# Output projection on 448 instead of 512 rows: two heads moved into the padding of the others by SBUF to SBUF transfers

## The chip, the cores and the metric

One core of one Trainium2 chip. The metric is the device time of one execution in microseconds (us), median of several. A ratio is the mean time of one kernel's fast runs over that of the other's fast runs of the same rounds, so it is not quite the ratio of the medians that are quoted beside it; the brackets after a ratio are its 95% interval.

## The reference

Two kinds of layer, each with a residual, applied as A, B, A, B to x of 2048 tokens by D = 448:

```python
def _A_ref(x, wqkv, wo):                     # on layernorm(x)
    H = 16; Dh = D // H                      # 16 heads of 28
    W, dil = 8, 2                            # 8 keys, every second token
    q, k, v = split(x @ wqkv)
    attn = softmax(where(mask, q . k[window] * Dh ** -0.5, -1e9))
    o = attn @ v[window]
    return o.reshape(B, S, D) @ wo           # the output projection

def _B_ref(x, w_gate, w_up, w_down):         # on layernorm(x), F = 1792
    return ((x @ w_gate) * (x @ w_up)) @ w_down
```

(cut and condensed; all data is bf16)

## The kernel before

The kernel keeps x in SBUF throughout. Heads have 28 rows, but a head sits in a slot of 32 partitions, so that the 16 heads fill four chunks of 128 partitions: `oT[128, 4, tokens]`. The four last rows of each slot are padding, and `wo_g` has zeros there. The output projection of a pair of 128-token blocks contracts half a chunk (64 rows) at a time; the two blocks work in the two halves of the array, crossed over after the first pass, so that each block gets all eight halves:

```python
wo_g = sb([128, 4, D], bf, "wo_g")
oT = sb([128, 4, HALF], bf, "oT")
...
memset("dve", wo_g[:], 0.0, "c_wo", 1000)
for j in range(4):
    dst = wo_g[32 * j:32 * j + DH, :, :]
    ...
# two blocks: 2 x 4 chunks x 2 halves = 16 matmuls of 64 x 128 by 64 x 448
twin_blocks(lambda w: ps[:, bk[w], 0:D],
            lambda w, c, lo: oT[lo:lo + 64, c, 128 * ((B + w) % 8):128 * ((B + w) % 8) + 128],
            lambda w, c, lo: wo_g[lo:lo + 64, c, :], ..., nd + WO, prio, bk)
```

The order of instructions on every engine is made when the kernel is built. A list scheduler simulates the engines with a table of durations and puts the instruction with the best priority next. The order then is fixed, and each engine is given its own instructions in it:

```python
def finish_of(self, key):
    ...
    if op.dma is not None:        # a transfer: the end of its issue, and its landing
        return max(o.end + o.lat for o in self.dgroup[(op.dma, op.mode)])
```

Two numbers of that table describe a transfer: what its issue takes on the queue, and its landing.

## Time and profile before

| | before |
|---|---|
| time, median (lowest to highest) of 3 | 394.73 us (393.76 to 395.34) |
| profiled span | 391.6 us |
| TensorE busy | 385.5 us, 98% |
| TensorE not busy | 391.6 - 385.5 = 6.1 us |
| granted clock, mean | 1.00 |
| issuing on the sync engine's queue, summed over the trace's records | 39.0 us of copies and loads, 98.9 us of transposes |

The prediction shows the lines that say what bounds it. One more view will be needed later, the busy time by stretches: start and end of the stretch, its length, the busy time of five engines (with the count of instructions), TensorE's granted clock, the share of the transfer engines, and GB/s. Of the kernel before:

```profile
30.00:40.00 10.00, 9.91 (x220) 5.34 (x218) 9.47 (x20) 8.38 (x17) 0.00 (x0) 1.00 0.08 20
60.00:100.00 40.00, 39.97 (x814) 23.48 (x811) 34.56 (x83) 27.14 (x55) 0.00 (x0) 1.00 0.23 43
```

TensorE has work all the time (9.91 of 10 and 39.97 of 40 us) and its clock is not lowered (1.00 in both). The weight loads are over by 30 us: the transfer engines' share falls to 0.08. By the trace's records the two matmuls of a pair start 3 to 4 ns apart and the next pair follows after 0.189 us at 448 columns and 0.216 us at 512 (97.4 to 98.4 us), while the record of one matmul is 349 or 376 ns long. From the last gate and up pair to the first matmul of an attention group it is 0.306 us where the next pair of its own kind follows after 0.21 us, so entering that mode costs about 0.09 us.

### The profile page before, as it was taken

The numbers are of one execution on the slowest core, as the hardware profiler recorded it, in microseconds if no ns is written. First come the engines' busy times: TensorE is split into PE (matmuls) and PEld (weight loads), VectorE is DVE, ScalarE is ACT, GpSimd is POOL, SyncE is SP. The second block draws the span as 40 slices with busy tenths as digits, with TensorE's granted clock in tenths as the row PEclk, the third lists the DMA queues.
The fourth block names the chain that finished last, engine by engine and source line by source line (L and its number), as shares of the span: only waits on it lengthen the run. The fifth ranks groups of instructions, "written<-read, shape, count | busy, mean of one in ns | idle before, by whom it ended". The sixth has DMA issues, their size and how long they took to land.

```text
span 391.6 us, 13910 instructions
## 1 busy us (share of the span) xinstructions
PE 385.5 (98%) x6142; PEld 214.1 (55%) x6142; DVE 271.0 (69%) x596; ACT 207.0 (53%) x398; POOL 7.8 (2%) x36
## 2 busy tenths in 40 slices
PE   8989999999999999999999999999999999999996
PEld 6645657655444544554556877444454544444674
DVE  5988999779957765784788644358932698467342
ACT  4788886578524745466742523368225772364130
POOL 6010000000000000000000000000000000000000
PEclk9999999999999999999999999999999999999999
DMA  8991143511221302210131151010150102402101
GB/s 274 300 288 34 21 92 32 97 24 28 49 49 28 77 7 56 42 28 13 17 49 27 30 95 29 25 23 8 26 118 5 23 7 56 88 3 20 31 25 47
DMA packets 53808, 22.47 MB, mean 57 GB/s; under 512 B 44837, under 2 KB 52853, under 8 KB 53749
## 3 DMA queue, kind: packets, MB, share of 16 engines
q1 hardware_dynamic: 52836, 19.47, 23.6%
q10 hardware_dynamic: 912, 2.12, 1.8%
q8 instruction: 48, 0.79, 0.8%
q14 instruction: 12, 0.09, 0.1%
HBM read 8.54 MB, written 2.71 MB: 29 GB/s over the span
## 4 chain that ended last, share of the span: by engine, by line
PE 98%; DVE 1%; issue 1%; DVEq 0%
PE ps L983 44%; PE ps L714 27%; PE ps L698 17%; PE ps L896 3%; PE ps L862 3%; PE ps L566 2%; PE ps L1004 1%; PE ps L660 1%; DVE xn_sb L651 0%; DVE x_sb L954 0%; DVEq L1084 0%; DVE O_sb L914 0%; DVE oT L937 0%; DVE O_sb L910 0%; DVE WQK L582 0%
## 5 line engine op out<-in xcount | busy, mean ns | idle before, releaser
L983 PE MATMUL ps<-xnTb,WGU 64*128 64x512 bf16 (+1 forms) x1960 | 180.4, 333 | 0.0
L983 PEld LDWEIGHTS ps<-xnTb,WGU 64*128 64x128 bf16 x1960 | 93.3, 94 | 72.9 <-ACT g_sb L989 1.5
L989 ACT ACTIVATE g_sb<-ps 128x512 bf16<-128x512 f32 (+1 forms) x140 | 71.4, 511 | 93.7 <-PE ps L983 93.1
L992 DVE TENSOR_TENSOR hT<-g_sb,ps 128x512 bf16<-128x512 bf16 (+1 forms) x140 | 79.2, 573 | 54.1 <-ACT g_sb L989 46.0
L714 PE MATMUL ps<-WD,hT 64*128 64x448 bf16 x840 | 84.0, 349 | 0.1
L714 PEld LDWEIGHTS ps<-WD,hT 64*128 64x128 bf16 x840 | 40.1, 94 | 36.9 <-DVE hT L992 0.7
L698 PE MATMUL ps<-xnTa,WQK 64*128 64x512 bf16 (+1 forms) x504 | 53.5, 353 | 0.3 <-DVE O_sb L914 0.2
L954 DVE TENSOR_TENSOR x_sb<-x_sb,ps 128x448 bf16<-128x448 bf16 x62 | 36.1, 612 | 25.2 <-PE ps L714 25.0
L630 DVE BATCH_NORM_STATS2 st<-x_sb 128x6 f32<-128x448 bf16 x64 | 37.4, 614 | 2.6 <-DMA x_sb<-in_A_x_dram 2.5
L869 ACT ACTIVATE E_sb<-ps 128x1024 bf16<-128x1024 f32 (+1 forms) x36 | 33.5, 980 | 9.8 <-PE ps L862 9.3
L750 ACT ACTIVATE qk<-ps 128x1024 bf16<-128x1024 f32 (+1 forms) x30 | 27.1, 921 | 19.3 <-PE ps L698 19.0
L651 DVE TENSOR_SCALAR xn_sb<-x_sb,mv,rstd 128x512 bf16<-128x512 bf16 (+1 forms) x64 | 33.6, 568 | 4.6 <-ACT rstd L635 4.6
L698 PEld LDWEIGHTS ps<-xnTa,WQK 64*128 64x128 bf16 x504 | 23.4, 94 | 24.0 <-ACT xnTa L666 0.8
L879 DVE TENSOR_TENSOR E_sb<-E_sb,MK 128x1024 bf16<-128x1024 bf16 (+2 forms) x40 | 23.9, 612 | 8.9 <-ACT E_sb L869 8.6
L714 PE MATMUL ps<-wo_g,oT 64*128 64x448 bf16 x256 | 29.1, 349 | 0.0
L633 ACT ACTIVATE lnv<-mv,eps_sb 128x2 f32<-128x2 f32 (+1 forms) x33 | 9.5, 293 | 30.5 <-DVE mv L632 30.2
L937 DVE TENSOR_TENSOR oT<-O_sb,R_sb 128x480 bf16<-128x480 f32 (+3 forms) x36 | 22.0, 625 | 3.4 <-ACT R_sb L926 3.1
L925 ACT ACTIVATE R_sb<-R_sb 128x480 f32<-128x480 f32 (+1 forms) x34 | 20.1, 601 | 5.7 <-DVE R_sb L924 5.7
L924 DVE STREAM_SHUFFLE R_sb<-O_sb 128x480 f32<-128x480 f32 (+1 forms) x34 | 22.6, 694 | 0.0
L698 PE MATMUL ps<-WV,xnTa 64*128 64x336 bf16 (+3 forms) x252 | 22.3, 304 | 0.2
L926 ACT ACTIVATE R_sb<-R_sb 128x480 f32<-128x480 f32 (+1 forms) x34 | 20.1, 602 | 0.3
L714 PEld LDWEIGHTS ps<-wo_g,oT 64*128 64x128 bf16 x256 | 12.3, 94 | 11.6 <-DVE oT L937 0.4
(47 smaller groups left out, 172.2 us busy)
## 6 DMA issues: line engine op xcount, KB each, us to landing
out_dram<-x_sb SPq DMA_DIRECT2D x15, 112.0 KB, 1.7
WD<-in_B_w_down_dram SPq DMA_DIRECT2D x2, 784.0 KB, 11.3
x_sb<-in_A_x_dram SPq DMA_DIRECT2D x3, 448.0 KB, 6.0
WGU<-in_B_w_up_dram SPq DMA_DIRECT2D x1, 896.0 KB, 18.0
WGU<-in_B_w_gate_dram ACTq DMA_DIRECT2D x1, 896.0 KB, 16.2
WGU<-in_B_w_up_dram SPq DMA_DIRECT2D x1, 672.0 KB, 17.8
WGU<-in_B_w_gate_dram ACTq DMA_DIRECT2D x1, 672.0 KB, 11.9
vt<-qk SPq DMA_DIRECT2D x42, 16.0 KB
```

Source lines behind the costliest of these rows:

```text
L630: sc.add("dve", one(lambda E, B=B: E.bn_stats(st6[:, B, :], x_sb[:, B, :]), ("bn", li, B)), 525.0, deps=[("x", li - 1, B)] + ([("xn", li - ...
L651: sc.add("dve", one(lambda E, B=B, dst=dst, src=src: E.tensor_scalar(dst, src, mv[:, B, 0:1], rstd[:, B:B + 1], ALU.subtract, ALU.mult), ( ...
L698: parts[0 if s < 3 else 1][1].append((lambda E, w=w, c=c, lo=lo, st=st, sp_=sp_: E.matmul(u["out"](w), u["lhs"](w, c, lo, lo + 64), u["rhs ...
L714: ins.append((lambda E, w=w, c=c, lo=lo, st=st, sp_=sp_: E.matmul(outs(w), lhs(w, c, lo), rhs(w, c, lo), start=st, stop=sp_), keys[w] if s ...
L750: return E.activation(dst, src, ACT.Copy) if hasattr(E, "activation") else E.tensor_copy(dst, src)
L869: return E.activation(E_sb[:, slot, 2 * hp:2 * hp + 2, 0:w], ps[:, b0:b0 + 2, 0:w], ACT.Exp, scale=SCALE)
L879: return E.tensor_tensor(e, e, m, ALU.mult)
L924: sc.add("dve", one(lambda E: E.stream_shuffle(R_sb[:, rs, 0:w], O_sb[:, os_, 0:w], [DH] * 32), ("Rs", li, qb)), dve_est(w) + 100.0, deps= ...
L954: sc.add("dve", one(lambda E: E.tensor_tensor(x_sb[:, B, :], x_sb[:, B, :], ps[:, bk[w], 0:D], ALU.add), ("x", li, B)), dve_est(D), deps=[ ...
L983: ins.append((lambda E, u=u, k=k, w=w: E.matmul(u["out"](w), WGU[64 * w:64 * w + 64, k, 128 * u["fc"]:128 * u["fc"] + 128], X[64 * w:64 * ...
L989: sc.add("act", one(lambda E, gs=gs, bk=bk: E.activation(g_sb[:, gs, 0:nt], ps[:, bk[0], 0:nt], ACT.Copy), ("G", li, j, fc)), act_est(nt), ...
L992: sc.add("dve", one(lambda E, gs=gs, bk=bk, fc=fc: E.tensor_tensor(hT[:, fc, hs, 0:nt], g_sb[:, gs, 0:nt], ps[:, bk[1], 0:nt], ALU.mult), ...
```

## The change

Intent: 448 rows need three and a half chunks, not four. Of chunk 3, half (two heads, 56 rows) is cut into pieces of 12 or 16 rows and moved by transfers into the padding rows of chunks 0 to 3 of the slots that remain; which half is moved depends on the parity w of the block, so that the two blocks of a pair still use different halves of the array. Each pair of blocks then takes 14 instead of 16 matmuls, 224 instead of 256 in all, for eight moves per pair, 128 in all. The core of the diff, with cuts marked:

```diff
+    MOVES = ((0, 0, 64, 16), (0, 32, 96, 16), (0, 64, 80, 12), (0, 96, 112, 12),   # w, slot, from row, rows
+             (1, 64, 0, 16), (1, 96, 32, 16), (1, 0, 16, 12), (1, 32, 48, 12))
-    wo_g = sb([128, 4, D], bf, "wo_g")
+    wo_g = sb([128, 2, 4, D], bf, "wo_g")            # one per parity, 16 loads instead of 4, no memset
-    twin_blocks(... oT[lo:lo + 64, c, ...], wo_g[lo:lo + 64, c, :], ..., nd + WO, prio, bk)
+    for n, (w, q, p0, k) in enumerate(MOVES):
+        dst = oT[q + DH:q + 32, 0:k // 4, m0 + 128 * w:m0 + 128 * w + 128]
+        src = oT[p0:p0 + k, 3, m0 + 128 * w:m0 + 128 * w + 128].unsqueeze(1)
+        sc.add("sp", one(lambda E, ...: E.dma_start(dst, src), ...), MVE, deps=nd, dma=f"d_m{p}", lat=MVL, ...)
+    for flip in (0, 1):
+        for c in range(4 - flip):                    # four halves, then three
+            ...
+    crossed(parts, [("OM", li, p)] + WO, prio, pe_cols(D), bk, "Yps")
+MVL = 2300.0                                         # the scheduler's table: landing of a move
+MVE = 330.0                                          # and its issue, ns
-PE_T = ("00", "01", "02", "03", "04")
+PE_T = ("00", "01", "02")                            # chunks of the first layer transposed on TensorE
...  (nearly every priority of the scheduler is new, the weights of the projection are loaded last,
...  some weight copies are bound to one engine, oT is a ring of 768 instead of 1024 tokens,
...  and the gate and up groups are kept in one fixed order)
```

More of the change, by code (lines that the diff above doesn't have):

```diff
@@ L28 @@
 MAIN = "R64"
-PE_T = ("00", "01", "02", "03", "04")
+PE_T = ("00", "01", "02")
 HEAD_LN = 5
-HEAD_P = (-53.71, -30.23, -20.33, -12.94, -19.33)
-HOLD_A = 1000.0
-HOLD_BA = 2000.0
-HOLD_BB = 500.0
+HEAD_P = (-25.07, -29.5, -27.33, -11.24, -8.12)
+HOLD_A = 0.0
+HOLD_BA = 1000.0
+HOLD_BB = 1000.0
 HOLD_N = 2
 S_EST = 270.0
-VX = 120.0
+VX = 0.0
 DPARTS = ((0, 7), (7, 14))
@@ L40 @@
 POOL_MASK = 0
-POOL_WQK = True
+WQK_ACT = ((0, 0), (0, 1), (2, 0))
 VFIRST = False
@@ L51 @@
 NBK = 8
-PR = {'AV': 8.84, 'rstd': -5.66, 'bn': 0.73, 'N': -2.82, 'Gps': -1.08, 'Tps': 16.85, 'H': 18.16, 'S': 10.61, 'VT': 19.61, 'Ex': 16.77, 'G': -2.93, 'xn': -6.19, 'QK': -6.56, 'Ddps': -26.52, 'V': 22.93, 'x': -0.84, 'lnv': -15.5, 'Oc': -6.51, 'Oa': -6.47, 'R': -19.3, 'VVps': 1.22, 'Yps': -25.3, 'PW': 58.69, 'T': -9.57, 'mv': 2.02, 'Rs': -2.57, 'Rl': 21.52, 'QKps': 4.71, 'E': -7.15, 'wqk': -9.31, 'wqp': -11.53}
-JP = {'A20': -3.02, 'B32': 16.28, 'B34': 16.21, 'A22': 20.13, 'B13': 2.73, 'A21': 6.27, 'B12': -2.81, 'A02': -0.21, 'A03': 4.03, 'B30': 4.3, 'B31': 8.23, 'B10': 21.86, 'B11': -14.15, 'A23': 29.86, 'A04': -0.79, 'B33': 153.62, 'A01': -5.33, 'B14': 4.53, 'A00': -24.6}
-XL = (2300.0, 2200.0, 4200.0, 5000.0, 5500.0)
+PR = {'lnv': 0.45, 'Yps': -0.46, 'Gps': 5.13, 'QK': 4.55, 'H': -5.95, 'R': -21.58, 'G': -8.35, 'VT': 8.79, 'S': -0.3, 'V': -1.49, 'Tps': 2.59, 'QKps': -8.74, 'T': 1.04, 'mv': -3.5, 'AV': -4.81, 'PW': 11.62, 'Oa': -19.68, 'bn': 1.23, 'N': -3.47, 'rstd': -11.91, 'Rl': -3.35, 'VVps': -4.87, 'x': -0.08, 'xn': -3.46, 'Ddps': -5.48, 'Ex': -6.97, 'E': 19.06, 'Rs': 1.63, 'Oc': 0.24, 'wqp': 2.97, 'wqk': 0.04}
+JP = {'A23': -34.68, 'B11': 4.55, 'B31': 13.93, 'A21': 15.34, 'A22': -41.14, 'B10': -17.89, 'A00': -1.57, 'B13': 1.34, 'B33': 15.35, 'A04': 3.4, 'A02': -1.01, 'A20': -93.26, 'B30': 0.09, 'B32': -5.05, 'A03': 22.53, 'B34': 1.96, 'A01': -0.42, 'B14': -9.92, 'B12': -2.11}
+XL = (3150.0, 4000.0, 4400.0, 5000.0, 5500.0)
 WVL = 5000.0
-STL = (2400.0, 2600.0, 2900.0, 2800.0)
-VONES_L = 18000.0
+STL = (2900.0, 3100.0, 3300.0, 3300.0)
+VONES_L = 15000.0
+MVL = 2300.0
+OW = 768
+WO_P = -43.2
+MVE = 330.0
 BL = (11000.0, 15000.0, 8000.0)
@@ L66 @@
 FILL = 30
-SEED = 190
+SEED = 557
 JITTER = 0
-ATT_P = 1.96
-A_CAP = 4
+ATT_P = 0.12
+A_CAP = 7
 B_CAP = 8
@@ L474, in build @@
     hT = sb([128, FC, 2, 512], bf, "hT")
-    oT = sb([128, 4, HALF], bf, "oT")
+    oT = sb([128, 4, OW], bf, "oT")
     ones32 = sb([128, 128], bf, "ones32")
@@ L488, in build @@
     sem_names += [f"d_t{li}_{j}" for li in range(4) for j in range(len(CH[li]))]
-    sem_names += [f"d_p{li}_{j}" for li in (0, 2) for j in range(len(CH[li]))] + [f"d_v{q}" for q in range(NQB)] + ["d_one", "d_stv"]
+    sem_names += [f"d_p{li}_{j}" for li in (0, 2) for j in range(len(CH[li]))] + [f"d_v{q}" for q in range(NQB)] + ["d_one", "d_stv"] + [f"d_m{p}" for p in range(NBLK // 2)]
     vt_all = nc.dram_tensor("vt", (256, S), bf, kind="Internal").ap()
@@ L498, in act_table_load, with plain_dma @@
         return E.add_instruction(atl)
-    def plain_dma(q, dst, src, key, sem, deps=(), lat=3000.0, prio=0.0, tmin=None):
-        sc.add(q, one(lambda E: E.dma_start(dst, src), key), {"sp": 520.0, "act": 500.0, "pool": 1000.0}[q], deps=deps, dma=sem, mode=0, lat=lat, prio=prio, tmin=tmin)
+    def plain_dma(q, dst, src, key, sem, deps=(), lat=3000.0, prio=0.0, tmin=None, est=None):
+        sc.add(q, one(lambda E: E.dma_start(dst, src), key), est or {"sp": 520.0, "act": 500.0, "pool": 1000.0}[q], deps=deps, dma=sem, mode=0, lat=lat, prio=prio, tmin=tmin)
     CH_ROWS = [0, 128, 192, 320]
@@ L533, in build @@
     memset("dve", eps_sb[:], EPS, "c_eps", 70)
-    memset("dve", wo_g[:], 0.0, "c_wo", 1000)
     sc.add("pool", one(lambda E: E.memset(ident[:], 1.0), "i_id"), 150, prio=-46)
@@ L574, in fn @@
                 return E.activation(dst, src, ACT.Copy) if hasattr(E, "activation") else E.tensor_copy(dst, src)
-            sc.add(("act", "dve", "pool") if POOL_WQK else ("act", "dve"), one(fn, ("wqk", c, w)), {"act": 470.0, "dve": 330.0, "pool": 600.0}, deps=[("stg", c), "c_wqk0"], prio=-28)
+            on_act = (c, w) in WQK_ACT
+            sc.add("act" if on_act else "dve", one(fn, ("wqk", c, w)), 560.0 if on_act else 300.0,
+                   deps=[("stg", c), "c_wqk0"] + ([("rstd", 0, int(WQK_ACT.index((c, w)) >= 1))] if on_act else []), prio=-28)
     for c in range(4):
@@ L588, in build @@
     ones_src = ones32[0:32, :].unsqueeze(1).to_broadcast([32, 16, 128])
-    plain_dma("sp", ones_dst, ones_src, ("vones",), "d_one", deps=["c_ones"], lat=VONES_L, prio=-40)
-    for j in range(4):
-        dst = wo_g[32 * j:32 * j + DH, :, :]
-        src = A_wo.rearrange("(c j e) d -> j e c d", c=4, j=4, e=DH)[j]
-        plain_dma("sp", dst, src, ("wo", j), "d_wo", deps=["c_wo"], lat=WOL, prio=-45)
+    plain_dma("sp", ones_dst, ones_src, ("vones",), "d_one", deps=["c_ones"], lat=3000.0, est=VONES_L, prio=-40)
+    MOVES = ((0, 0, 64, 16), (0, 32, 96, 16), (0, 64, 80, 12), (0, 96, 112, 12), (1, 64, 0, 16), (1, 96, 32, 16), (1, 0, 16, 12), (1, 32, 48, 12))
+    for j in range(8):
+        src = A_wo.rearrange("(c j e) d -> j e c d", c=4, j=4, e=DH)[j % 4]
+        plain_dma("sp", wo_g[32 * (j % 4):32 * (j % 4) + DH, j // 4, :, :], src, ("wo", j), "d_wo", lat=WOL, prio=WO_P)
+    for n, (w, q, p, k) in enumerate(MOVES):
+        r0 = DH * (12 + p // 32) + p % 32
+        plain_dma("sp", wo_g[q + DH:q + 32, w, 0:k // 4, :], A_wo[r0:r0 + k, :].rearrange("(r c) d -> r c d", r=4), ("wo", 8 + n), "d_wo", lat=WOL, prio=WO_P)
     for n, (k0, k1) in enumerate(KP):
@@ L599, in build @@
     WDR = [("wd", 0), ("wd", 1)]
-    WO = [("wo", j) for j in range(4)]
+    WO = [("wo", j) for j in range(16)]
     rings = {n: [None] * k for n, k in (("xn", NXN), ("o", NO), ("v", NV), ("v2", NV2), ("e", NE if PAIRED else 2 * NE), ("r", NR), ("g", NG))}
@@ L630, in ln_chunk @@
                 sc.add("dve", one(lambda E, B=B: E.bn_stats(st6[:, B, :], x_sb[:, B, :]), ("bn", li, B)), 525.0,
-                       deps=[("x", li - 1, B)] + ([("xn", li - 1, B)] if li else []), prio=prio)
+                       deps=[("x", li - 1, B)] + ([("xn", li - 1, B)] if li else []) + ([("mv", 0, 0)] if (li, B) == (0, 1) else []), prio=prio)
                 sc.add("dve", one(lambda E, B=B: E.bn_aggr(mv[:, B, :], st6[:, B, :]), ("mv", li, B)), 100.0, deps=[("bn", li, B)], prio=prio - 0.1)
@@ L927, in norm @@
         war = []
-        for B in range(tok // 128, (tok + nq - 1) // 128 + 1):
-            if B >= 8:
-                war.append(("Y", li, B - 8))
-            elif li >= 2:
-                war.append(("Y", li - 2, B + 8))
-        cut = [tok] + [HALF] * (tok < HALF < tok + nq) + [tok + nq]
+        g0 = S * (li // 2)
+        for p in range(tok // 256, (tok + nq - 1) // 256 + 1):
+            q = p + 8 * (li // 2) - OW // 256
+            if q >= 0:
+                war += [("Y", 2 * (q // 8), 2 * (q % 8)), ("Y", 2 * (q // 8), 2 * (q % 8) + 1)]
+        cut = [tok] + [t - g0 for t in range(0, 2 * S, OW) if tok < t - g0 < tok + nq] + [tok + nq]
         ins = []
@@ L936, in fn @@
             def fn(E, a=a, z=z):
-                return E.tensor_tensor(oT[:, :, a % HALF:a % HALF + z - a], O[:, :, a - tok:z - tok], R_sb[:, rs, 0:w].rearrange("p (h n) -> p h n", h=4)[:, :, a - tok:z - tok], ALU.mult)
+                m = (a + g0) % OW
+                return E.tensor_tensor(oT[:, :, m:m + z - a], O[:, :, a - tok:z - tok], R_sb[:, rs, 0:w].rearrange("p (h n) -> p h n", h=4)[:, :, a - tok:z - tok], ALU.mult)
             ins.append((fn, ("N", li, qb) if z == cut[-1] else None))
@@ L947, in y_blocks @@
                 nd.append(("N", li, qb))
-        twin_blocks(lambda w: ps[:, bk[w], 0:D], lambda w, c, lo: oT[lo:lo + 64, c, 128 * ((B + w) % 8):128 * ((B + w) % 8) + 128], lambda w, c, lo: wo_g[lo:lo + 64, c, :],
-                    (("Y", li, B), ("Y", li, B + 1)), [range(4)], [[]], nd + WO, prio, bk)
+        p, m0 = B // 2, (128 * B + S * (li // 2)) % OW
+        for n, (w, q, p0, k) in enumerate(MOVES):
+            dst = oT[q + DH:q + 32, 0:k // 4, m0 + 128 * w:m0 + 128 * w + 128]
+            src = oT[p0:p0 + k, 3, m0 + 128 * w:m0 + 128 * w + 128].unsqueeze(1)
+            sc.add("sp", one(lambda E, dst=dst, src=src: E.dma_start(dst, src), ("OM", li, p) if n == 7 else None), MVE, deps=nd, dma=f"d_m{p}", mode=li, lat=MVL, prio=prio + PR.get("OM", 0.0) * (n < 7))
+        parts = []
+        for flip in (0, 1):
+            ins = []
+            for c in range(4 - flip):
+                for h in (0, 1):
+                    w, lo = h ^ flip, 64 * h
+                    ins.append((lambda E, w=w, c=c, lo=lo, flip=flip: E.matmul(ps[:, bk[w], 0:D], oT[lo:lo + 64, c, m0 + 128 * w:m0 + 128 * w + 128], wo_g[lo:lo + 64, w, c, :],
+                                                                           start=c == 0 and flip == 0, stop=c == 2 and flip == 1),
+                                ("Y", li, B + w) if c == 2 and flip == 1 else None))
+            parts.append((flip, ins, []))
+        crossed(parts, [("OM", li, p)] + WO, prio, pe_cols(D), bk, "Yps")
         for w in range(2):
@@ L960, in build @@
     hslot_users = {}
+    gu_ops = []
     LASTB = [(int(b[1]), int(b[2])) for b in SEQ if b[0] == "B"][-1]
@@ L984, in b_chunk @@
                                                                  X[64 * w:64 * w + 64, k, c0:c0 + nt], start=k == 0, stop=k == 6), u["keys"][w] if k == 6 else None))
-            sc.add("pe", ins, 7 * pe_cols(nt), deps=u["deps"] + tdeps, mode=MAIN, prio=prio, acquire=u["bk"])
+            gu_ops.append(sc.add("pe", ins, 7 * pe_cols(nt), deps=u["deps"] + tdeps, mode=MAIN, prio=prio, acquire=u["bk"], after=gu_ops[-1] if gu_ops else None))
             for u in us[m:m + 1]:
```

## The prediction

> **What bounds the kernel now.** I read first the page's busy rows, then the chain of work that ended last, then the costliest groups, and last the waits.
>
> ```profile
> span 391.6 us, 13910 instructions
> PE 385.5 (98%) x6142; PEld 214.1 (55%) x6142; DVE 271.0 (69%) x596; ACT 207.0 (53%) x398; POOL 7.8 (2%) x36
> ...
> PE 98%; DVE 1%; issue 1%; DVEq 0%
> PE ps L983 44%; PE ps L714 27%; PE ps L698 17%; PE ps L896 3%; PE ps L862 3%; PE ps L566 2%; PE ps L1004 1%; PE ps L660 1%; DVE xn_sb L651 0%; DVE x_sb L954 0%; DVEq L1084 0%; DVE O_sb L914 0%; DVE oT L937 0%; DVE O_sb L910 0%; DVE WQK L582 0%
> ...
> L714 PE MATMUL ps<-wo_g,oT 64*128 64x448 bf16 x256 | 29.1, 349 | 0.0
> ```
>
> TensorE is busy 385.5 of 391.6 us, and the chain that ended last runs on it for 98% of the span. Nearly all of that chain is matmuls in order, one after the other. So a matmul taken away shortens the run by its slot, and a wait added on another engine costs nothing until TensorE runs out of other work. The group that the change touches is the output projection, wo_g with oT: 256 matmuls. Its column of idle time before is 0.0: TensorE does not wait for it today.
>
> The mean of 349 ns is latency and not cost, because two matmuls of 64 rows run beside each other in the two halves of the array. The cost is in the chain in order of time, whose columns are start, length and what:
>
> ```profile
> 13.75 1.00 PE ps L660 x16
> ...
> 82.29 0.61 PE ps L896 x64
> 82.91 1.62 PE ps L983 x14
> ...
> 97.58 0.76 PE ps L714 x8
> 98.34 1.51 PE ps L983 x14
> 99.85 0.76 PE ps L714 x8
> ```
>
> Eight output-projection matmuls, four pairs, take 0.76 us (0.757 by the starts, 98.34 less 97.58, is the same): 0.19 us a pair. A PE transpose of 128x128 takes 1.00/16 = 62.5 ns. Fourteen gate and up matmuls take 1.51 us among others of their kind and 1.62 us after an attention group, so leaving a 32-row or 128-row mode costs about 0.11 us.
>
> The waits of the sync engine's queue, which issues the transfers, and what one small transfer costs there:
>
> ```profile
> SPq L770 <- DMA vt<-qk: 13.1, 6, 2.2
> L759 SPq DMA_DIRECT2D vt<-qk x49: 254/308/654, 39.8 to 303.2; - x49
> L654 SPq DMA_TRANSPOSE xnTa<-xn_sb x16: 1190/1260/1269, 92.0 to 236.3; - x16
> DMA to landing us min/median/max: 2.4/3.0/4.7
> ```
>
> A small copy takes 0.308 us to issue (middle figure of min, median, max) and 13.1/6 = 2.2 us from the last issue until its reader may go on. A transpose takes 1.26 us to issue and 2.4 to 4.7 us to land.
>
> [...] 1.51/7 = 216 ns a pair. [...] the changed kernel makes TensorE wait for all eight moves of a pair of blocks, so their full latency lies between the normalised heads and the projection.
>
> **The change, part by part.** A head has 28 rows in a slot of 32, so 448 rows fill four chunks of 128 with 64 padding rows.
>
> 1. Fewer projection matmuls. The two blocks of a pair each use four chunks in two halves: 2 x 4 x 2 = 16 matmuls. Now the heads of half a chunk (56 rows) lie in the padding of the others, so each block uses seven halves: 14. There are 8 pairs in each of 2 attention layers, so 16 x 2 = 32 matmuls or 16 pairs fewer: 16 x 0.189 = 3.03 us. The instruction order of the two kernels confirms 256 and 224. All of this lies on the engine that sets the end: -3.0.
>
> 2. Fewer transposes on TensorE. The list of chunks that it transposes loses the last two of the first layer, six blocks of four: 64 becomes 40 matmuls, 24 x 62.5 ns = -1.5 us. In return six DMA transposes are issued.
>
> 3. Mode switches. In the order of instructions I count 74 changes between tile modes before and 72 after: about -0.2 us.
>
> 4. The end. Before, the last work is a pair of blocks: matmuls end at 388.3 us, two 448-column additions follow (1.15 us together), then the store. In the changed order the last work is one block in two 224-column halves, whose addition takes 0.39 us today. About -0.7 us.
>
> 5. The moves. 8 x 8 x 2 = 128 small copies. By the issue cost above 128 x 0.308 = 39 us on the sync queue, spread over the run; six transposes add 6 x 1.26 = 7.6 us, and sixteen instead of four weight loads some 5. Today the queue issues for about 130 us of 391 (49 copies at 0.31, 48 transposes at 1.29, 27 at 1.23, some 40 others at 0.5), so it goes to about 180, under half. For one pair of blocks the moves put 8 x 0.308 + 2.2 = 4.7 us between normalisation and projection. The changed order fills this: between the end of an attention group and its first projection other matmuls are placed. In the interleaved part nothing of it should reach TensorE. In the first 60 us, where little gate and up work is ready, some may.
>
> 6. Retuned order. Nearly every priority and hold value is new, so the whole order differs, not just the projection. VectorE loses the 0.81 us memset of wo_g, which ran while it waited for the input anyway: 0. The first layer now starts with the V projection, and weight copies are bound to fixed engines. The first real work before starts at 9.9 us, after warm-up matmuls, and needs input, layer norm and transposes that the change doesn't speed up: 0, with the largest uncertainty here.
>
> Sum: -3.0 - 1.5 - 0.2 - 0.7 = -5.4 us. Can the retuning win more? The streaming time of all real matmuls by the slots above (588 pairs of 512 columns at 216 ns in gate and up, and so on) is about 370 us, an estimate of mine; 74 switches at 0.09 to 0.11 make 7. Between 9.9 and 388.3 lie 378.4 us. So only some 1 to 2 us of true idling are there to win.
>
> I add back 0.7 us for new waits, and get -4.7: 394.7 - 4.7 = 390.0 us, 1.2% less.
>
> **Rivals.**
> - The move takes the place of the removed work: TensorE waits for the moves where no other matmul is ready. For it: 4.7 us more latency on each of 16 pairs, an in-order sync queue that today already waits for VectorE at many places, and transposes of 1.2 us that a move can stand behind. Against it: no idle time before projection today, and an order made with the moves in it. If four of the sixteen pairs cost 1.5 us each, the gain is gone: 394 to 396 us.
> - The head gets worse: the six DMA transposes stand in the same queue behind the weight loads, which keep the engines full until about 29 us (the page's DMA row shows 8, 9, 9 tenths, then 1), and behind twelve more loads. By my count of slots the changed order needs these chunks at about 37 us. If the loads end after 35 us, TensorE idles 1 to 4 us: 391 to 394 us.
> - The move is hidden wholly and the new order also removes idle time: -6 to -7 us: 388 us.
> - VectorE or ScalarE becomes the bound: at 69% and 53%, with almost unchanged work, no.
>
> **Range and chances.** The sum of matmuls is counted, so the centre is safe to about a microsecond; the waits go one way. 387.3 to 393.8 us should hold it 8 times in 10. Faster by over 2% means under 386.8 us, which needs more than the counted savings together: 0.07. Slower by over 2% means over 402.6 us, some 13 us of new waits: 0.03. Within 2%: 0.90.
>
> **What would show it right or wrong.** Right: 224 projection matmuls at an unchanged 0.76 us for eight, TensorE's busy time near 381 us, idle before the projection near zero, sync issues near 180 us. The moves' landing should be 2 to 3 us. Wrong on waits: TensorE's waits name the transfer oT<-oT before the projection, or the idle time moves to gaps in slices 3 to 6. Wrong on the head: the first 60 us finish less work than before, with waits for xnTa from a transfer. Wrong on the tail: the last matmul ends more than 3 us before the end of the span. A median under 387 us would say that the order had more idle time in it than I counted.

## The result, and the profile after

| | before | after |
|---|---|---|
| time, median (lowest to highest) of 4 each | 395.03 us (393.76 to 396.06) | 424.97 us (423.65 to 427.45) |
| ratio | | 1.0767 [1.0703, 1.0831], slower |
| profiled span | 391.6 us | 421.9 us |
| TensorE busy | 385.5 us | 389.7 us |
| TensorE not busy | 6.1 us | 32.2 us |
| issuing of copies and loads on the sync queue | 39.0 us | 131.0 us |
| issuing of transposes on it | 98.9 us | 115.9 us |

The page of the changed kernel: span, busy row, the chain that ended last, and the projection's group (busy, mean ns of one, then idle before it and what ended most of it):

```profile
span 421.9 us, 13941 instructions
...
PE 389.7 (92%) x6086; PEld 214.9 (51%) x6086; DVE 278.9 (66%) x610; ACT 198.8 (47%) x383; POOL 6.6 (2%) x33
...
PE 75%; SPq 8%; DMA 6%; DVE 5%; issue 3%; ACT 2%; DVEq 0%
...
L968 PE MATMUL ps<-wo_g,oT 64*128 64x448 bf16 x224 | 28.7, 373 | 16.3 <-DMA oT<-oT 16.3
```

Before, TensorE held 98% of the chain and the projection group's idle column was 0.0. Now TensorE holds 75%, the sync queue (SPq) and transfers hold 14%, and the projection waits 16.3 us, all of it for the moved rows. There are 56 fewer matmuls (6086 for 6142), but they are busy for longer; why is in the clock, below.

The moves on their queue (min, median, max ns of one issue, and when), the first eight in the queue's timeline (start, length, what), and the chain in order of time around the first projection (start, length, what):

```profile
L961 SPq DMA_DIRECT2D oT<-oT x128: 622/629/837, 44.3 to 386.5; - x128
```

```profile
44.30 5.46 SPq L961 DMA_DIRECT2D oT<-oT  x8
```

```profile
45.10 0.63 SPq L961
45.73 0.04 issue
45.78 0.63 SPq L961
...
49.13 1.73 DMA oT<-oT
...
50.91 0.93 PE ps L968 x8
```

A move takes 0.629 us to issue and 0.04 us pass between two, so 0.67 us each and 8 x 0.67 = 5.4 us for a pair of blocks. The chain's transfer of 1.73 us begins with the issue of the last move, at 49.13 us; that issue ends at 49.76 us, and the rows are there 1.1 us later. So 5.4 + 1.1 = 6.5 us lie between the first issue and the projection (6.4 to 6.8 us in 14 of the 16 groups), where the prediction had 4.7 us and the scheduler's table 8 x 0.33 + 2.3 = 4.9 us. The landing takes half of what was assumed (2.2 and 2.3 us after the last issue); the issue takes twice as long.

The busy time by stretches of the changed kernel, columns as before:

```profile
30.00:40.00 10.00, 6.78 (x168) 3.23 (x168) 5.45 (x11) 4.05 (x6) 0.00 (x0) 0.83 0.95 117
60.00:100.00 40.00, 31.94 (x623) 20.67 (x615) 25.03 (x59) 16.49 (x36) 0.00 (x0) 0.91 0.37 55
```

In 60 to 100 us TensorE now does 623 matmuls where it did 814, and the granted clock is 0.91. The same view in slices of 2 us shows how the two hang together, around one wait for moved rows (TensorE's records end at 83.1 us and begin again at 86.07):

```profile
84.00:86.00 2.00, 0.00 (x0) 0.00 (x0) 0.55 (x2) 0.00 (x0) 0.00 (x0) 1.00 0.05 11
86.00:88.00 2.00, 1.93 (x18) 1.13 (x20) 0.00 (x0) 0.00 (x0) 0.00 (x0) 0.64 1.06 120
88.00:90.00 2.00, 2.00 (x16) 1.04 (x14) 0.42 (x1) 0.39 (x1) 0.00 (x0) 0.51 0.83 97
```

After a stop of 3.0 us the clock is at half for some 3.4 us (by the two slices, (0.36 + 0.49) x 2 / 0.5), and the matmuls issued then take twice as long: in the trace's records, pairs of 448 columns begin 0.373 us apart from 88.6 to 89.7 us and 0.189 us apart from 90.0 us on. So this wait was paid for twice: the stop, and slow matmuls after it. The trace's clock records show five such stretches of 3.413 us in the changed kernel, each worth 3.413 / 2 = 1.7 us, and none within the span of the kernel before. Each begins within 0.5 us of the end of a stop of 1.7 to 3.2 us (the third at 86.56 us).

TensorE's waits, in us in total, times, longest:

```profile
PE ps L968 <- DMA oT<-oT: 16.3, 11, 3.0
PE ps L904 <- issue: 4.9, 2, 3.2
PE ps L904 <- DMA v_sb<-vt: 2.9, 1, 2.9
```

The first is the wait for the moves. The second is none that the profile can name: it shows nothing that TensorE waited for, and TensorE did not go on, 3.2 us of it in one place at 32 us, before the first move was issued. It is not the moves' doing, and gets experiments of its own.

### The profile page after: what moved, and what is told of

It is laid out like the page before. It is cut to its first block, busy times and chain, and to the rows that moved or that the text cites. A ratio compares the mean times of both kernels' runs of the same rounds, so it can differ in the third digit from the quotient of the medians.

```text
span 421.9 us, 13941 instructions
## 1 busy us (share of the span) xinstructions
PE 389.7 (92%) x6086; PEld 214.9 (51%) x6086; DVE 278.9 (66%) x610; ACT 198.8 (47%) x383; POOL 6.6 (2%) x33
## 4 chain that ended last, share of the span: by engine, by line
PE 75%; SPq 8%; DMA 6%; DVE 5%; issue 3%; ACT 2%; DVEq 0%
PE ps L1007 36%; PE ps L706 15%; PE ps L722 15%; SPq L961 8%; PE ps L968 5%; DMA oT<-oT 4%; PE ps L904 2%; PE ps L870 2%; PE ps L1028 1%; DMA x_sb<-in_A_x_dram 1%; DMA xnTb<-xn_sb 1%; DVE oT L946 1%; DVE hT L1016 1%; DMA v_sb<-vt 1%; DVE st L638 1%
## 5 line engine op out<-in xcount | busy, mean ns | idle before, releaser
L1007 PE MATMUL ps<-xnTb,WGU 64*128 64x512 bf16 (+1 forms) x1960 | 180.6, 336 | 1.4 <-DMA xnTb<-xn_sb 1.2
L1007 PEld LDWEIGHTS ps<-xnTb,WGU 64*128 64x128 bf16 x1960 | 96.2, 95 | 73.2 <-issue 2.5
L722 PE MATMUL ps<-WD,hT 64*128 64x448 bf16 x840 | 85.1, 354 | 0.0
L722 PEld LDWEIGHTS ps<-WD,hT 64*128 64x128 bf16 x840 | 41.6, 95 | 39.5 <-issue 2.4
L968 PE MATMUL ps<-wo_g,oT 64*128 64x448 bf16 x224 | 28.7, 373 | 16.3 <-DMA oT<-oT 16.3
L758 ACT ACTIVATE qk<-ps 128x1024 bf16<-128x1024 f32 (+1 forms) x24 | 22.1, 935 | 21.7 <-PE ps L706 21.7
L968 PEld LDWEIGHTS ps<-wo_g,oT 64*128 64x128 bf16 x224 | 10.0, 97 | 29.5 <-DMA oT<-oT 21.1
L946 DVE TENSOR_TENSOR oT<-O_sb,R_sb 128x480 bf16<-128x480 f32 (+11 forms) x39 | 21.9, 589 | 3.5 <-ACT R_sb L934 3.4
L706 PE MATMUL ps<-WV,xnTa 64*128 64x336 bf16 (+3 forms) x252 | 23.2, 314 | 1.0 <-ACT E_sb L877 0.8
L933 ACT ACTIVATE R_sb<-R_sb 128x480 f32<-128x480 f32 (+1 forms) x34 | 19.6, 597 | 5.1 <-DVE R_sb L932 5.0
L758 DVE CAST qk<-ps 128x1024 bf16<-128x1024 f32 (+1 forms) x12 | 13.0, 1086 | 10.7 <-PE ps L706 10.7
```

The lines of the kernel that those rows point to most:

```text
L706: parts[0 if s < 3 else 1][1].append((lambda E, w=w, c=c, lo=lo, st=st, sp_=sp_: E.matmul(u["out"](w), u["lhs"](w, c, lo, lo + 64), u["rhs ...
L722: ins.append((lambda E, w=w, c=c, lo=lo, st=st, sp_=sp_: E.matmul(outs(w), lhs(w, c, lo), rhs(w, c, lo), start=st, stop=sp_), keys[w] if s ...
L758: return E.activation(dst, src, ACT.Copy) if hasattr(E, "activation") else E.tensor_copy(dst, src)
L968: ins.append((lambda E, w=w, c=c, lo=lo, flip=flip: E.matmul(ps[:, bk[w], 0:D], oT[lo:lo + 64, c, m0 + 128 * w:m0 + 128 * w + 128], wo_g[l ...
L1007: ins.append((lambda E, u=u, k=k, w=w: E.matmul(u["out"](w), WGU[64 * w:64 * w + 64, k, 128 * u["fc"]:128 * u["fc"] + 128], X[64 * w:64 * ...
```

## The experiments

Theory A: the moves take twice the assumed issue time on a queue that issues them one after the other (0.67 us apart), for which the order leaves no room; undone, the counted gain of 5 us appears. Rivals: the moves cost TensorE time whatever the order (contention, clock); the cost comes from the retuned order and its head and not from the moves; the moves are slow only because source and destination differ in shape.

Wherever a run leaves out moves or weights, its result is wrong; the matmuls, their shapes and their number stay the same. Lines of code shift by a few from kernel to kernel: the projection is L968 or L976, attention times v L904 or L912, gate and up L1007 or L1015.

### 1. The changed kernel without its moves

The order is made with all moves in it, and then they are not issued.

```diff
+SKIP = tuple(range(8))
-sc.add("sp", one(lambda E, ...: E.dma_start(dst, src), ...), MVE, deps=nd, ...)
+sc.add("sp", one(None if n in SKIP else lambda E, ...: E.dma_start(dst, src), ...), MVE, deps=nd, ...)
```

> The changed kernel with every engine's order kept, but none of the 128 moves issued (the result is wrong on purpose; the projection waits for the normalised heads instead). Theory A, the moves are the whole loss: it comes to what the prediction counted, 388 to 393 us against 395 before, with TensorE's clock back at 1.0. Theory B, the new order itself is bad (first 60 us, six more DMA transposes, fixed weight copies): it stays above 405 us. In between, the two share the loss.

Measured: 395.03 us (393.98 to 395.33), ratio 0.9988 [0.9938, 1.0038]. Page, waits and stretches:

```profile
span 392.2 us, 13805 instructions
...
PE 381.1 (97%) x6086; PEld 220.3 (56%) x6086; DVE 277.9 (71%) x610; ACT 198.4 (51%) x383; POOL 6.5 (2%) x33
```

```profile
PE ps L912 <- issue: 3.2, 1, 3.2
```

```profile
30.00:40.00 10.00, 6.79 (x170) 3.30 (x168) 5.61 (x11) 4.27 (x6) 0.00 (x0) 0.83 0.78 120
60.00:100.00 40.00, 39.02 (x770) 29.98 (x768) 35.33 (x83) 25.43 (x54) 0.00 (x0) 1.00 0.37 59
```

The moves cost the 30 us: from this run to the changed kernel the span grows by 29.7 us, of which 32.2 - 11.1 = 21.1 us are idle time of TensorE and 389.7 - 381.1 = 8.6 us are the same 6086 matmuls being busy for longer. Most of these 8.6 us are the lower clock: the clock records have one stretch of half clock in this run and five in the changed kernel, and four more are 4 x 1.7 = 6.8 us. But the other half of theory A fails: without the moves the time is that of the kernel before, not 390. TensorE's work shrank by 385.5 - 381.1 = 4.4 us, close to the counted saving, and its idle time grew from 6.1 to 11.1 us. Most of that is in the head: 3.2 us in the stretch from 30 to 40 us, in one stop that the profile puts down to "issue". The half clock after that stop (0.83 in the mean of these 10 us) costs another 1.7 us, which the 381.1 us contain; stop and half clock together are 4.9 us, about what is missing.

### 2. Half of the moves

```diff
-SKIP = tuple(range(8))
+SKIP = (1, 3, 5, 7)
```

> As the run before, but four of each eight moves are issued, in the same places. Wrong result on purpose. Theory A by issue time: each group then holds the queue for 4 x 0.67 = 2.7 us, which is what the order was made for (8 x 0.33), so nearly nothing is lost: 389 to 396 us. If instead the landing (1.7 us after the last issue) or the wait as such costs the time, half of the 30 us stays: 405 to 412 us.

Measured: 395.41 us (395.03 to 395.71), ratio 1.0005 [0.9947, 1.0063]. The first four moves cost 0.4 us against the run without any, which is within the noise, the second four 30 us. Linear contention is out. It fits the room that the order leaves: four moves take 4 x 0.67 + 1.1 = 3.8 us until their rows are there (3.7 to 3.9 us in 15 of the 16 groups), under the 4.9 us that the order was made for; eight take 6.5 us, 1.6 us over it, at each of 16 pairs. (The 1.7 us of landing in the expectation begins with the last issue and not after it.)

### 3. Moves with source and destination of one shape

```diff
-src = oT[p0:p0 + k, 3, m0 + 128 * w:m0 + 128 * w + 128].unsqueeze(1)
+src = oT[p0:p0 + 4, 0:k // 4, m0 + 128 * w:m0 + 128 * w + 128]
```

(wrong rows)

> All eight moves at their places, but each takes four source partitions with three or four pieces of 128, the same shape as its destination, in place of 12 or 16 source partitions with one piece (wrong result on purpose). If the unequal shapes make the issue dear, the issue falls from 0.63 us to about 0.31 us as for the copies of qk to DRAM, and the time to 390 to 396 us. If any SBUF to SBUF copy costs 0.63 us to issue, nothing changes: 422 to 428 us.

Measured: 423.61 us (422.58 to 427.94), ratio 1.0736 [1.0659, 1.0814]; a move took 0.646 us to issue. The difference of shapes is not what makes it slow.

### 4. The order made again with the measured issue cost

```diff
-MVE = 330.0
+MVE = 670.0
```

> The changed kernel with the true issue cost of a move, 670 ns in place of 330, given to the list scheduler that fixes the order. The result is right. If the loss came from an order made with a wrong number, most of it goes: 395 to 408 us. If the queue is simply too full or the extra latency can't be hidden, it stays within 2% of 425 us.

Measured, correct: 408.3 us (407.02 to 409.18), ratio 1.0326 [1.0272, 1.038]. That is 0.3 us over the range that I gave. TensorE's waits:

```profile
PE ps L904 <- issue: 4.9, 1, 4.9
PE ps L1007 <- DMA xnTb<-xn_sb: 4.4, 1, 4.4
PE ps L968 <- DMA oT<-oT: 1.8, 2, 1.5
```

One number in the table is worth 17 us: the wait for moved rows goes from 16.3 to 1.8 us. In its place stands a wait for a transposed chunk, whose transfer stands in the same queue behind moves. The priorities were still those found for the wrong number.

### 5. Forms of transfer, one beside the other

In two pairs of blocks, six of the eight moves were replaced by other forms, for their issue times alone. 423.71 us.

```diff
+FORMS = (move, oT[0:16] -> DRAM, DRAM -> 16 rows, oT[4:8] -> 4 rows, oT[16:32] -> 16 rows,
+         oT[32:33] -> 1 row, oT[64:68] x 4 pieces -> DRAM, move)
-lambda E, ...: E.dma_start(dst, src)
+FORMS[n] if u in (9, 10) else FORMS[0]
```

> The changed kernel; in two of its sixteen groups of moves six of the eight take other forms (wrong result on purpose), each on its own tile: 16 rows SBUF to DRAM; 16 rows DRAM to SBUF; 4 rows, 16 rows and 1 row of 256 bytes SBUF to SBUF; 4 rows of 4 pieces SBUF to DRAM. If two SBUF ends make the issue dear, the three SBUF to SBUF forms take 0.6 us or more whatever their rows, and the three with a DRAM end about 0.3 us. If the 256-byte pieces make it dear, all six take 0.6 us. If the number of pieces does, the forms of 1 and 4 rows are cheap and those of 16 dear.

The issue times (min, median, max ns), in the order issued:

```profile
L966 SPq DMA_DIRECT2D zd<-oT x2: 434/436/437, 222.9 to 228.2; - x2
L967 SPq DMA_DIRECT2D ones<-in_A_wo_dram x2: 406/410/415, 223.3 to 228.7; - x2
L968 SPq DMA_DIRECT2D ones<-oT x2: 622/630/639, 223.8 to 229.2; - x2
L969 SPq DMA_DIRECT2D ones<-oT x2: 567/570/572, 224.5 to 229.8; - x2
L970 SPq DMA_DIRECT2D ones<-oT x2: 585/586/586, 225.1 to 230.4; - x2
L971 SPq DMA_DIRECT2D zd<-oT x2: 683/688/693, 226.1 to 231.1; - x2
```

Of 16 rows, a copy with one end in DRAM (L966, L967) takes 0.41 to 0.44 us and one with both in SBUF (L969) 0.57 us. The number of rows matters little: 0.63, 0.57 and 0.59 us for 4, 16 and 1 row (L968 to L970). The last line does not fit: four rows of four pieces into DRAM took 0.69 us. The move after it took 0.69 too instead of 0.63 us, so these two may show something of the neighbour; two records each do not settle it. What holds: every SBUF to SBUF form measured costs 0.57 us or more, and the prediction's 0.308 us came from copies into DRAM.

### 6. Without moves, with the six transposes back on TensorE

Is it the new DMA transposes of the first layer, in the queue behind the weight loads, that cost the head its 3.2 us?

```diff
 SKIP = tuple(range(8))
-PE_T = ("00", "01", "02")
+PE_T = ("00", "01", "02", "03", "04")
```

> As the run without moves, but TensorE transposes all five chunks of the first layer as in the kernel before, so the six early DMA transposes are gone (wrong result on purpose; the order is made anew). If these transposes keep the transfer engines full past 30 us and so delay TensorE's instructions (the gap of 3.2 us inside one group near 32 us), the gap falls under 1 us and the time to 388 to 392 us, in spite of 1.5 us more work. If the gap has another cause, the time stays at 394 to 397 us.

Measured: 399.84 us (397.98 to 400.43), ratio 1.0106 [1.004, 1.0171]. A miss: slower than with the DMA transposes, and a stop of 3.1 us put down to "issue" was there again.

### 7 and 8. The moves on GpSimd's queue

```diff
-sc.add("sp", one(lambda E, ...: E.dma_start(dst, src), ...), MVE, deps=nd, ...)
+sc.add("pool", one(lambda E, ...: E.dma_start(dst, src), ...), MVE, deps=nd, ...)
-MVE = 330.0
+MVE = 1100.0
```

> The changed kernel with all moves issued from GpSimd, idle otherwise, at 1.1 us of issue in the scheduler's table, so the sync queue is free of them. Right result. If the loss is the sync queue's time for the moves and what stands behind them there, the time falls below the 408 us of the run with the true cost, to 396 to 404 us. If it is the latency of the chain (8 x 1.1 + 2.3 = 11 us here, against 7), it rises to 408 us or more.

Measured, correct: 409.13 us (408.43 to 409.25), ratio 1.0345 [1.0295, 1.0396]. An issue took 0.574 us there, half of the 1.1 us that I had put in the table and that no run had measured. The sync queue was free of moves, and yet it came out like run 4: TensorE waited 8.1 us for a transposed chunk (7.7 us in one place, near 70 us). Run 8 is the same with all five chunks transposed on TensorE:

> Both: moves from GpSimd, and TensorE transposes all five chunks of the first layer. Right result. If the head's gap comes from the DMA transposes, it gains some 3 us on the run with GpSimd alone: 392 to 401 us. If not, it is 1 to 2 us slower than that run by its own extra transposes.

Measured, correct: 410.99 us (408.69 to 412.36), ratio 1.039 [1.0329, 1.0452]. Both miss the gain that I hoped for, and the times fall where the expectations put a long chain (run 7) and the extra transposes (run 8). A long chain is not what run 7 shows: its eight moves took 5.6 to 8.0 us from the first issue to the landing in 15 of 16 groups, not 11, and no wait of TensorE names them. A free queue alone does not help while the order is made for a wrong number.

### 9, 10 and 11. The stop in the head

TensorE stops in the changed kernel and in runs 1, 2, 4, 7, 10 and 11 after exactly its 474th matmul, and in runs 6 and 8 after its 473rd, though what comes next there differs. The trace's transfer records have a queue of instructions alone, in packets of 16,384 bytes, which by its size I take to be TensorE's:

```profile
q8 instruction: 48, 0.79, 0.8%
```

6086 matmuls and as many weight loads are 12,172 instructions; over 48 packets that is about 254 each, so by this estimate one packet feeds TensorE with some 127 matmuls. The stops lie on that grid: in all sixteen traces, each of the 30 stops over 0.4 us in the first 70 us that are put down to "issue" stands within two matmuls of the 220th, 347th, 474th, 601st, 728th or 1109th, and these are whole multiples of 127 apart. Theory B: in the head, with the transfer engines full of weights, such a packet comes too late. Three edits were to move the loads, all on run 1 with its order otherwise untouched:

```diff
+# 9: the w_down loads from the sync queue's start to ScalarE's queue at about 42 us
+late = [o for o in sc.order["sp"] if o.dma in ("d_wd0", "d_wd1")]
+sc.order["sp"] = [o for o in sc.order["sp"] if o not in late]
+sc.order["act"][n:n] = late
+# 10: the 16 loads of wo_g ahead of the w_down loads;  11: both
+early = [o for o in sc.order["sp"] if o.dma == "d_wo"]
```

> The run without moves once more, with every engine's order kept, but the two loads of the down weights (1.57 MB), first needed near 88 us, leave the sync queue at the start and are issued from ScalarE's queue near 42 us (wrong result only because there are no moves). Theory: in all variants so far TensorE stops at its 474th matmul near 32 us, whatever that matmul is, because the third 16 KB block of its instructions is fetched only when the weight loads have drained. Then the block is fetched some microseconds earlier, the gap of 3.2 us and the half clock after it go, and the time falls from 395.0 to 388.5 to 391.5 us. If the gap has another cause, it stays, with 394 to 397 us.

> The run without moves (wrong result for that reason), every engine's order kept, but the sixteen loads of the output weights stand ahead of the gate, up and down weights on the sync queue, as the four loads did in the kernel before. Theory: late loads of 896-byte rows keep few transfer engines busy past 30 us and hold up TensorE's instruction block and what stands behind them. Then the long gap at the 474th matmul (3.2 us) shrinks under 1 us and the time falls from 395.0 to 389 to 392 us. If the number of bytes alone decides, the gap stays and so do 394 to 397 us.

> As the run before, and the down weights from ScalarE's queue near 42 us as well. If both the place and the bytes matter, TensorE has no long gap at an end of an instruction block before 40 us, and the time is 388 to 391 us. If the run before already removed the gap, this one is equal to it within 1.5 us. If neither matters, 394 to 398 us.

Measured: run 9 397.57 us (393.66 to 399.44), ratio 1.0019 [0.9933, 1.0104]; run 10 399.53 us (396.97 to 400.32), 1.0094 [1.0041, 1.0147]; run 11 394.51 us (393.56 to 397.51), 1.0001 [0.995, 1.0053]. All three miss. The stop stayed or moved: 4.1 us at the 474th matmul in run 10, 2.4 us in run 11; in run 9 there was none there, but one of 1.7 us after the 220th and one of 2.2 us after the 347th matmul, and others beside them (its profiled execution took 398.69 us). The loads were moved, but not lessened.

### 12 and 13. All priorities searched again for the measured cost

The scheduler's priorities were searched anew with the true costs in the table, once with the moves on GpSimd's queue at 600 ns and once on the sync queue at 670 ns, both correct.

```diff
-MVE = 330.0
+MVE = 600.0        # 12: on GpSimd's queue;   13: 670.0, on the sync queue
-PR = {'lnv': 0.45, 'Yps': -0.46, ...}
+PR = {'lnv': 45.38, 'Yps': -21.98, ...}        # and HEAD_P, JP, HOLD_BA, HOLD_BB, ATT_P, A_CAP
```

> The changed kernel, correct, with the eight moves of a group on GpSimd's queue, their cost in the scheduler's table at 600 ns an issue and 2100 ns a landing (what the earlier GpSimd run measured as 570 and 1600 to 2100), and all priorities searched anew for that table, which the earlier corrected runs (408.3, 409.1) did not have. Theory A (the loss is the order having been made for a wrong issue cost): the wait for moved rows goes under 3 us in all and the time is 393 to 399; what stays over 390 is the stop at TensorE's 474th matmul in the head. Rival (the moves themselves cost TensorE time, whatever the order): 405 to 412, as in the two corrected runs.

> The same with the moves left on the sync queue at 670 ns an issue and the priorities searched anew. Theory A: 396 to 403, a few us above the GpSimd one, since the queue also carries the 49 copies for the transposed values; the wait for moved rows under 4 us. Rival (the moves cost TensorE time whatever the order): 406 to 412, no better than the corrected table alone (408.3).

Measured: run 12 401.76 us (399.54 to 402.65), ratio 1.0149 [1.0102, 1.0196]; run 13 403.08 us (401.8 to 403.63), ratio 1.0194 [1.0162, 1.0226]. Run 12 is 2.8 us over the range that I gave, run 13 at its upper edge; by the 2% rule run 12 is the same as before and run 13 unclear. TensorE's longest waits of run 12, then of run 13:

```profile
PE ps L904 <- issue: 5.3, 2, 4.6
PE ps L904 <- DMA v_sb<-vt: 3.2, 1, 3.2
PE ps L870 <- issue: 2.6, 2, 2.3
PE ps L968 <- DMA oT<-oT: 0.6, 1, 0.6
```

```profile
PE ps L904 <- issue: 4.4, 1, 4.4
PE ps L968 <- DMA oT<-oT: 2.3, 1, 2.3
```

The moves do not cost TensorE much by themselves: with an order made for them, all 128 are issued at 0.57 or 0.63 us, and the wait for moved rows is 0.6 or 2.3 us. Of the 30 us, 22 to 23 were the order. What is left over 395 us is mainly in the head, where the stops put down to "issue" (7.9 us in run 12) are larger than before.

### 14. Run 1 with about half of the weights loaded

```diff
-plain_dma("sp", WGU[64:128, k0:k1, :], B_w_up[64 * k0:64 * k1, :]...)          # gate likewise
+plain_dma("sp", WGU[64:128, k0:k1, 0:F // 2], B_w_up[64 * k0:64 * k1, 0:F // 2]...)
-plain_dma("sp", WD[:, 7 * n:7 * n + 7, :], B_w_down[...])
+plain_dma("sp", WD[:, 7 * n:7 * n + (7, 1)[n], :], B_w_down[...])               # 8 of 14 blocks
-128 * u["fc"]:128 * u["fc"] + 128                                              # and the loaded columns are read twice
+128 * (u["fc"] % 7):128 * (u["fc"] % 7) + 128
```

> The order of the changed kernel without its moves (the run that took 395.0), but only half of each gate and up weight and four sevenths of the down weight are loaded, and the matmuls read those columns twice: wrong on purpose, same matmuls in the same order and shapes, 2.3 of 4.8 MB less to load in the head. Theory B (the stop of 3.2 us at the 474th matmul is the third 16,384-byte block of TensorE's instructions coming late behind the weight loads): the transfer engines are free by some 22 us, the stop at the 474th matmul is under 0.5 us, and the time is 389.5 to 392.5. Rival (the stop has to do with the order of the changed kernel, not with the loads): it stays at 2.4 to 4.9 us, and the time is 394 to 396.

Measured: 394.91 us (392.52 to 395.31), ratio 0.998 [0.994, 1.0019]. In the profiled execution the stop is gone from its place, but the gain does not come. (That execution is the fastest of the four, 392.52 us; the others took 394.83 to 395.31 us and were not looked into.) From the transfer records, the third packet of TensorE's instructions in the trace:

| | its fetch begins | TensorE then at matmul | TensorE is through with the 474th | stop there |
|---|---|---|---|---|
| before | 30.05 us | 454 | 32.7 us | none |
| run 1 | 32.37 us | 474, standing | 32.0 us | 3.2 us |
| run 14 | 30.99 us | 376 | 35.0 us | none |

In run 1 the next four packets are fetched 49 to 112 matmuls ahead of need. With about half of the loads this third one is too, 474 - 376 = 98 ahead, where run 1 had it at 0 and the kernel before at 474 - 454 = 20: that speaks for theory B. But it is no clean proof, since TensorE came to the 474th matmul 3 us later than in run 1, and at that pace a late packet would have done as well. Timeline of TensorE (start, length, what, and idle before it), then the stretches of run 14:

```profile
28.16 0.32 PE L878 MATMUL ps<-qk 28*64 28x64 bf16 x15 [0.83 <-issue]
28.42 4.77 PE L714 MATMUL ps<-xnTa,WQK 64*128 64x512 bf16 x28
```

```profile
20.00:30.00 10.00, 8.16 (x150) 3.49 (x152) 6.59 (x25) 7.21 (x15) 0.56 (x3) 0.91 1.14 160
30.00:40.00 10.00, 10.00 (x260) 4.89 (x258) 8.16 (x14) 7.11 (x12) 0.00 (x0) 0.92 0.34 28
```

A shorter stop stands after the 347th matmul instead, 127 matmuls earlier, and the clock goes to half after it: 28 matmuls take 4.77 us, where 14 pairs at the 0.216 us that a pair of 512 columns took in the kernel before would be 3.0. Besides, TensorE's named waits of run 14 sum to 6.2 us (2.5 us in the kernel before), none over 1.2 us: the new order has small gaps in its head, and with the large one removed the others remain.

## Why the prediction was wrong

Predicted 390.0 us, in 387.3 to 393.8; measured 424.97 us. By its own steps:

- Steps 1 to 4 (fewer matmuls, transposes, mode switches, a shorter end: -5.4 us) held as far as the traces tell them apart. There are 224 projection matmuls, eight still take 0.76 us in the chain where they don't wait, TensorE's busy time without the moves is 381.1 us (predicted near 381), and the end after the last matmul is 421.9 - 419.5 = 2.4 us where it was 391.6 - 388.3 = 3.3 us. The mode switches (-0.2 us) have no measurement of their own.
- Step 5 (the moves) is the one that failed: "128 x 0.308 = 39 us on the sync queue" and "8 x 0.308 + 2.2 = 4.7 us". The 0.308 us was taken from copies whose other end is in DRAM, since the profile of before has no SBUF to SBUF copy at all; the move measured 0.629 us to issue and 0.67 us in a row. The landing after the last issue (2.2 us, again from copies into DRAM) was 1.1 us, so the 4.7 us are 5.4 + 1.1 = 6.5 us. The queue issues for 131.0 + 115.9 = 247 us, not 180.
- The sentence built on it, "In the interleaved part nothing of it should reach TensorE", failed by more than the number: this order, with its fixed sequence, hid what it was made for and little beyond. Half the moves cost 0.4 us (run 2), all of them 30 us (from run 1 to the result); the correct number alone in the table brings back 17 us (run 4), a new search 22 to 23 us (runs 12, 13). Of the 29.7 us, 21.1 are stops and 8.6 longer busy time, of which some 6.8 are the half clock after stops, a term that the prediction did not have.
- Step 6 (the head, "0, with the largest uncertainty here") was off by some 5 us: without the moves the time is 395.0 us and not 390. TensorE's work shrank by 4.4 us and its idle time grew by 5.0. The largest piece is 3.2 us after the 474th matmul, with 1.7 us of half clock after it. That the packet of instructions is late there is in the records (run 1: its fetch begins at 32.37 us, TensorE stands from 32.0 us); that the weight loads hold it up is supported by run 14 and not settled. When this stop went, the median time stayed, and in the profiled execution smaller gaps and a half clock stood in its place: the loss seems to belong to the new order's head as a whole, and no run got it back.
- Of the rivals, "the move takes the place of the removed work" named the right wait but sized it at 6 us for four of sixteen pairs (measured: 11 waits, 16.3 us); "the head gets worse" was right in size (1 to 4 us) and wrong in cause: it named the six DMA transposes, which run 6 clears of the stop. VectorE and ScalarE were not the bound, as said.

What stays open: what delays TensorE's instructions in the head; what in a transfer's form sets its issue time (run 5 has one form that breaks the pattern), and whether a better order could bring the changed layout under 395 us. None of the versions that I ran does: the best correct one takes 401.8 us.

## What to carry to other kernels

An issue cost read from a profile belongs to the form of transfer that it was read from (here 0.308 us for copies into DRAM, 0.629 us for the moves): if the change brings in a form that the profile does not have, say so, and put twice the cost into the sum to see whether the schedule would bear it. In this kernel, whose order is fixed at build time, moves that kept within the time of the table cost nothing (run 2), and moves that took 1.6 us longer at 16 places cost 30 us, somewhat more than the product, since five stretches of half clock came with the stops, 1.7 us each. A saving of 1% that comes with a new order of everything has to be checked in the head first, where loads, instruction fetches and a lowered clock met here.

## What the traces showed of transfers, clock and instruction fetches

- Issue and landing: eight small moves took 5.4 us to issue and had landed 1.1 us after the last issue; 128 of them held the queue for 86 us (128 x 0.67).
- Landing and issue by form: the copies into DRAM had landed 2.2 us after the last issue; the moves within SBUF took half of it (1.1 us after the last issue, 1.7 us with that issue). An issue took 0.57 to 0.65 us for SBUF to SBUF copies on the sync queue, 0.574 us for the moves on GpSimd's, 0.41 to 0.44 us for 16 rows from or to DRAM, 0.308 us for the copies of the kernel before.
- Half clock: stops of 1.7 to 3.2 us came with a stretch of it in the changed kernel, stops of 2.0 us (71 to 73 us) and 2.4 us (236 to 238 us) did not, and in run 14 it came after a stretch whose longest stop was 0.83 us. In the clock records of the changed kernel the half rate begins 9, 17, 24, 33 and 39 times 3.413 us, the length of one such stretch, after the first rise of the clock, so where a stop falls on this grid may count as well as its length; no run tests that.
- Instruction fetches: 48 packets of 16,384 bytes, by the estimate above about 127 matmuls with their weight loads each. In the head of the variants TensorE stopped for 2.4 to 4.9 us after the 474th matmul, with the third fetch of the trace beginning at 32.37 us in run 1, when TensorE already stood. What makes such a fetch come late was not shown.
